# Query chunks of batches 3 to 7 transposed by DMA in a fused linear-attention and FFN kernel

## The chip, the cores and the metric

The kernel runs on one core of a Trainium2 chip. The metric is the device time of one execution, in microseconds (us). Five runs of the kernel before give a median of 259.1 us (258.8 to 259.48). Besides them there is one profiled execution; every duration below comes from it.

## The reference

A cosformer attention (linear attention with cosine and sine weights) is followed by a multiplicative feed-forward network:

```python
def phi(x, c, s):                      # q, k, v: (8 batches, 8 heads, 576, 64)
    r = np.maximum(x, 0.0)
    return np.concatenate([r * c, r * s], axis=-1)
q_p, k_p = phi(q, cos_w, sin_w), phi(k, cos_w, sin_w)
kv = np.einsum('bhsf,bhsd->bhfd', k_p, v)
z = np.sum(k_p, axis=2)
num = np.einsum('bhsf,bhfd->bhsd', q_p, kv)
den = np.einsum('bhsf,bhf->bhs', q_p, z)[..., None] + 1e-06
x = (num / den).transpose(0, 2, 1, 3).reshape(4608, 512)
out = ((x @ w1) * (x @ w2) @ w3) @ w_out          # widths 1024, 1024, 1024, 512
```

## The kernel before, in words

The 576 tokens of a batch are cut into five chunks, four of 128 rows and chunk 4 of 64. `order_of(b)` gives their order: 0, 1, 2, 3, 4 for even batches and 4, 0, 1, 2, 3 for odd ones. The FFN runs over the 4608 tokens in nine tiles of 512; w3 and w_out are multiplied into one matrix `w34b` during the first of them.

The main loop runs over the FFN tiles, t = 0 to 8; I call one turn a stage. `ffn_groups(t)` is a generator which emits TensorE work of tile t in up to 24 pieces of four matmuls (some 0.9 us each): eight pairs of products with w1 and w2 (L438, evacuated at L475 on ScalarE and L479 on VectorE), then four output blocks (L484, L490, stores at L423). After each piece the units of the slot of that number are emitted, so the slots set the order in which the other work joins each engine's queue. The schedule is manual: each engine executes its instructions in the order in which they were emitted, and waits on semaphores where one needs another's result.

In stage t (from t = 2 on; stages 0 and 1 have slot tables of their own) three batches are in work:

- Batch t+3 is loaded by DMAs that GpSimd issues (L112, L114), with a cast to bf16. K, q and v are put into slots 1, 8 and 15.
- Batch t+2 gets its features: `prep_k`, `prep_q`, `prep_v` for each chunk, spread over slots 0 to 22, in stage 1 (batch 3) over slots 6 to 23. The cosine half is made on VectorE (L251), the sine half on ScalarE (L255), the copy of v on GpSimd (L275).
- Batch t+1 gets its attention (`attention_at`): `kv_chunk` in slots 0 to 4 (L283), then for each chunk `num` (L341, with the normalization on VectorE, L349 to L351) and `x_tr` in slots 6, 8, 11, 14, 17. For batches 2 and later `x_tr` is a DMA transpose that SP issues (L373); it writes the normalized rows into `xT`, the FFN's input.

`num` needs the query features with the feature dimension on the partitions: `qpT`. There are two ways to get there. By TensorE: `q_tr` makes eight transposes into PSUM (L314, one for each head), and VectorE copies the result to `qpT` (L316). That happens in the batch's own attention stage, in slots 2, 4, 7, 10 and 13 of stage b-1. By DMA: `prep_q` issues a transpose from SP (L269) right after the chunk's features, in stage b-2. `dma_q(b)` lists the chunks of batch b that go by DMA; `attention_at` gives the others to `q_tr`.

Before the change `dma_q` gives no chunk for batches 0 to 2, chunks 2 and 3 for batch 3, chunks 2, 3, 4 for batches 4 and 6, chunks 1, 2, 3 for batch 5, and all five for batch 7. SP's queue holds these transposes and those of `x_tr`, in the order of the slots.

Because batches have 576 rows and FFN tiles 512, `xT` of tile t takes rows from two batches. Tile 3 takes the last rows of batch 2 and chunks 4, 0 and 1 of batch 3; tile 4 takes chunks 2 and 3 of batch 3 and chunks 0 and 1 of batch 4; tile 5 the other three of batch 4 and chunks 4 and 0 of batch 5.

`qpT` has two buffers (L243), and so have the feature tiles and the loaded tiles; `xT` has three.

Of the kernel before, what the change touches and what calls it, by code (L numbers as in the profile page):

```python
# [68 lines left out]
def kernel(  # L69
# [12 lines left out]
    B = q.shape[0]  # L82
# [141 lines left out]
    def order_of(b):  # L224

        return [0, 1, 2, 3, 4] if b % 2 == 0 else [4, 0, 1, 2, 3]

    def dma_q(b):

        return order_of(b)[5 if b < 3 else 3 if b == 3 else 2 if b < B - 1 else 0:]  # L230

    feat = {}

# [31 lines left out]
    def prep_q(b, c):  # L265
        features(b, feat_of(b)[1], raw[b, "q"], c)
        if c in dma_q(b):
            R = ROWS[c]
            nc.sync.dma_start_transpose(out=att_of(b)["qpT"][:, :, ds(columns_of(b, c), R)],  # L269
                                        in_=feat[b][1][:R, c].rearrange("p h f -> p (h f)"))  # L270
# [110 lines left out]
    def attention_at(b, slots, kv, tr, nu, xt):  # L381

        each = list(enumerate(order_of(b)))
        for i, c in each:
            slots[kv[i]].append(lambda c=c, i=i: kv_chunk(b, c, i))
            if c not in dma_q(b):
                slots[tr[i]].append(lambda c=c: q_tr(b, c))
        for i, c in each:
            if xt[i] > nu[i]:
                slots[xt[i]].append(lambda c=c: x_tr(b, c))  # L390
        for i, c in each:
            slots[nu[i]].append(lambda c=c: num(b, c))
            if xt[i] == nu[i]:
                slots[xt[i]].append(lambda c=c: x_tr(b, c))
# [238 lines left out]
```

## Time and profile before

| | |
|---|---|
| median of five runs | 259.1 us (258.8 to 259.48) |
| the profiled execution | 259.03 us, its span 257.3 us |
| mean granted TensorE clock | 0.995 |
| transposes by TensorE for `qpT` (L314) | 184, 23 chunks, with eight more at L327 |
| copies PSUM to `qpT` (L316) | 20 on VectorE, 12.4 us in total |
| DMA transposes to `qpT` (L269) | 16, issue 1.26 us, 2.7 / 4.1 / 6.1 us to landing (min/median/max) |
| DMA transposes to `xT` (L373) | 30, issue 1.19 us, 2.3 / 3.1 / 7.7 us to landing |
| DMA moved | 37.1 MB, mean 144 GB/s |

In what follows the span starts at 0. PE is TensorE's matmul side, PEld its weight loads, DVE VectorE, ACT ScalarE, POOL GpSimd, SP SyncE. A busy row of PE includes the tail of its pipeline, so the time that a group of matmuls costs is read from the start of the group to the start of the next one. "To landing" is the time from the issue of a DMA to its completion. The DMA share of a stretch can exceed 1, since packets of one engine overlap.

### The profile page before, as it was taken

Reading aid. Unit: us, or ns where it says so; the run is one execution under the profiler, and the core shown is the slowest. Engines: PE = TensorE matmul, PEld = TensorE weight load, DVE = VectorE, ACT = ScalarE, POOL = GpSimd, SP = SyncE. Lnnn points to the kernel's source line nnn. Section 1 sums busy time; section 2 is a strip of 40 time slices with the busy share of each in tenths; the row PEclk is TensorE's granted clock in tenths of the full one; section 3 lists DMA queues with packets and bytes.
Section 4 is the critical chain, followed back from the end, with each engine's and each line's share of the span. In section 5 each row is a group of like instructions: output and inputs, shape, how many; then the busy total and the mean of one; then the engine's idle time right before and its main releaser. Section 6 shows DMA issues by size and latency. Waiting matters only on the chain.

```text
span 257.3 us, 5053 instructions
## 1 busy us (share of the span) xinstructions
PE 247.0 (96%) x1934; PEld 135.2 (53%) x1967; DVE 146.1 (57%) x346; ACT 128.0 (50%) x219; POOL 85.5 (33%) x147
## 2 busy tenths in 40 slices
PE   8889999999999999999999999999999999999992
PEld 3478555656565455446544654555455544444441
DVE  6775655847879549824871787278526614303310
ACT  2675316727966546555655465646523233323321
POOL 7665144530760483048305900610230031022000
PEclk9999999999999999999999999999999999999998
DMA  7999999999999599999999999826490252024025
GB/s 195 183 194 203 207 206 201 198 199 198 237 160 138 102 201 171 173 171 162 192 150 181 176 195 135 179 50 131 94 194 13 54 123 70 0 44 122 1 44 120
DMA packets 68025, 37.10 MB, mean 144 GB/s; under 512 B 35617, under 2 KB 64545, under 8 KB 68001
## 3 DMA queue, kind: packets, MB, share of 16 engines
q0 software_dynamic: 35488, 27.20, 66.0%
q1 hardware_dynamic: 32352, 9.44, 21.9%
q8 instruction: 15, 0.25, 0.4%
q10 hardware_dynamic: 160, 0.13, 0.2%
q14 instruction: 10, 0.07, 0.1%
HBM read 38.80 MB, written 9.44 MB: 187 GB/s over the span
## 4 chain that ended last, share of the span: by engine, by line
PE 89%; DMA 3%; ACT 2%; issue 2%; DVE 1%; POOL 1%; ACTq 0%; POOLq 0%
PE ffnps L438 47%; PE ffnps L484 22%; PE ffnps L218 5%; PE pst L314 4%; PE pnum L341 4%; PE pnum L283 3%; DMA qs<-in_q_dram 3%; PE pst L206 1%; PE pst L377 1%; ACT kp L255 1%; POOL vs L120 0%; ACT qpT L317 0%; PE ffnps L501 0%; ACT osb L503 0%; DVE xblk L351 0%
## 5 line engine op out<-in xcount | busy, mean ns | idle before, releaser
L479 DVE TENSOR_TENSOR abT<-asb,ffnps 128x512 bf16<-128x512 bf16 x68 | 46.4, 682 | 64.1 <-PE ffnps L438 57.6
L438 PE MATMUL ffnps<-xT,w1b 128*128 128x512 bf16 (+2 forms) x312 | 74.3, 357 | 0.9 <-DVE xT L379 0.3
L438 PE MATMUL ffnps<-xT,w2b 128*128 128x512 bf16 (+2 forms) x306 | 73.2, 356 | 0.5
L475 ACT CAST asb<-ffnps 128x512 bf16<-128x512 f32 x68 | 39.8, 586 | 63.0 <-PE ffnps L438 55.5
L484 PE MATMUL ffnps<-w34b,abT 128*128 128x512 bf16 x273 | 63.3, 379 | 0.4
L423 POOL DMA_DIRECT2D out_dram<-osb x42 | 22.3, 536 | 120.1 <-ACT osb L490 120.1
L438 PEld LDWEIGHTS <-w1b 128*128 128x128 bf16 x320 | 28.9, 98 | 27.5 <-issue 0.8
L484 PEld LDWEIGHTS <-abT 128*128 128x128 bf16 x280 | 26.5, 98 | 30.3 <-DVE abT L479 0.4
L438 PEld LDWEIGHTS <-w2b 128*128 128x128 bf16 x320 | 27.5, 97 | 22.7
L490 ACT COPY osb<-ffnps 128x512 f32<-128x512 f32 x35 | 20.5, 586 | 37.8 <-PE ffnps L484 36.7
L255 ACT ACTIVATE qp<-qs,sinv 128x512 bf16<-128x512 bf16 (+2 forms) x40 | 28.1, 717 | 1.2 <-DMA qs<-in_q_dram 1.2
L351 DVE TENSOR_TENSOR xblk<-pnum,den 128x512 bf16<-128x512 f32 (+1 forms) x39 | 26.9, 691 | 1.4
L255 ACT ACTIVATE kp<-ks,sinv 128x512 bf16<-128x512 bf16 (+1 forms) x35 | 24.9, 722 | 0.0
L341 PEld LDWEIGHTS <-qpT 128*128 128x128 bf16 x320 | 15.1, 98 | 8.8 <-DVE xblk L351 0.9
L251 DVE TENSOR_SCALAR qp<-qs,cosv 128x512 bf16<-128x512 bf16 (+1 forms) x40 | 18.2, 462 | 0.5 <-DMA qs<-in_q_dram 0.5
L275 POOL COPY va<-vs 128x512 bf16<-128x512 bf16 (+1 forms) x30 | 18.4, 644 | 0.0
L341 PE MATMUL pnum<-kvs,qpT 128*128 128x65 bf16 x312 | 16.4, 194 | 0.4 <-DVE kvs L289 0.3
L283 PEld LDWEIGHTS <-kp 128*128 128x128 bf16 x280 | 12.7, 98 | 5.2
L316 DVE COPY qpT<-pst 128x1024 bf16<-128x1024 bf16 (+1 forms) x20 | 12.4, 618 | 4.8 <-PE pst L314 4.7
L218 PE MATMUL ffnps<-woutb,w3T 128*128 128x512 bf16 x61 | 15.0, 379 | 0.1
L314 PEld LDWEIGHTS <-qp 128*128 128x128 bf16 x184 | 12.0, 98 | 4.7
L283 PE MATMUL pnum<-va,kp 128*128 128x65 bf16 x280 | 14.1, 193 | 0.0
(81 smaller groups left out, 178.8 us busy)
## 6 DMA issues: line engine op xcount, KB each, us to landing
out_dram<-osb POOLq DMA_DIRECT2D x16, 256.0 KB, 3.8
out_dram<-osb POOLq DMA_DIRECT2D x24, 128.0 KB, 3.1
qs<-in_q_dram POOLq DMA_DIRECT2D x9, 256.0 KB, 8.0
ks<-in_k_dram POOLq DMA_DIRECT2D x7, 320.0 KB, 7.7
qs<-in_q_dram POOLq DMA_DIRECT2D x7, 320.0 KB, 8.2
vs<-in_v_dram POOLq DMA_DIRECT2D x7, 320.0 KB, 10.0
w3b<-in_moe_w_dram POOLq DMA_DIRECT2D x8, 256.0 KB, 12.7
ks<-in_k_dram POOLq DMA_DIRECT2D x7, 256.0 KB, 8.3
```

The source lines that it names most:

```text
L218: nc.tensor.matmul(acc[:, :], lhsT=w3T[:, lc, :], rhs=woutb[:, lc, :], start=(lc == 0), stop=(lc == 7))
L255: nc.scalar.activation(out=dst[:R, c, 0:n, D:F], in_=src[:R, 0:n, c, :], func=ACTF.Relu, scale=sinv[:R, at:at + 1], bias=0.0)
L283: nc.tensor.matmul(kvt[:, h // 4, ds((h % 4) * 65, 65)], lhsT=kp[:, c, h, :], rhs=va[:, c, h, 0:D + 1], start=(i == 0 and h % 4 == 0), sto ...
L314: nc.tensor.transpose(pst[:, h, :], qp[:, c, h, :], identb[:])
L341: nc.tensor.matmul(nt[:, h // 4, ds((h % 4) * 65, 65)], lhsT=qpT[:, h, ds(at, 128)], rhs=kvs[:, h, :], start=True, stop=True)
L351: nc.vector.tensor_tensor(out=xblk[rows], in0=n4[:, :, :, 0:D], in1=den[rows].unsqueeze(3).to_broadcast([R, 2, 4, D]), op=ALU.mult)
L423: on.dma_start(out=rows[:, :, cols], in_=osb[64 * i:64 * i + rows.shape[0], :, cols])
L438: nc.tensor.matmul(out, lhsT=w[:, kc, ts(jc, 128)], rhs=x[:, kc, tok], start=(kc == 0), stop=(kc == 3))
L475: nc.scalar.copy(out=asb[:], in_=aT[:, :])
L479: nc.vector.tensor_mul(out=abT[:, jc, :], in0=asb[:], in1=bT[:, :])
L484: nc.tensor.matmul(ops[:, :], lhsT=abT[:, jc, ts(ms, 128)], rhs=w34b[:, jc, :], start=(jc == 0), stop=(jc == 7))
L490: nc.scalar.copy(out=osb[:, ms % 2, :], in_=ops[:, :])
```

## The change

`dma_q` lists all five chunks for batches 3 to 7. Batches 0 to 2 stay with TensorE.

```diff
     def dma_q(b):
 
-        return order_of(b)[5 if b < 3 else 3 if b == 3 else 2 if b < B - 1 else 0:]
+        return order_of(b)[5 if b < 3 else 0:]
```

So nine chunks change their path: 4, 0 and 1 of batch 3, 0 and 1 of batch 4, 4 and 0 of batch 5, 0 and 1 of batch 6. For each of them `prep_q` issues a DMA transpose on SP in stage b-2, and `q_tr` with its eight transposes and its VectorE copy drops out of stage b-1. Nothing else is edited.

## The prediction

> **What bounds the kernel now.** I read the page first (busy times, then the row of granted clock), then the busy times of TensorE (PE) stage by stage, then single pieces of PE's timeline, and last the landings of the transposes that SP issues.
>
> The page:
>
> ```profile
> span 257.3 us, 5053 instructions
> PE 247.0 (96%) x1934; PEld 135.2 (53%) x1967; DVE 146.1 (57%) x346; ACT 128.0 (50%) x219; POOL 85.5 (33%) x147
> ...
> PEclk9999999999999999999999999999999999999998
> DMA  7999999999999599999999999826490252024025
> ```
>
> PE is busy in 96% of the span at a granted clock of nine tenths or more throughout; no other engine comes near. The DMA row is the only other full one, up to about slice 27 (174 us), and that is the stretch in which the change adds DMA work.
>
> Busy times in the five stages t = 2 to 6 (a row is: stretch, length, PE, PEld, DVE, ACT, POOL, clock, DMA share, GB/s). I took the borders from the first matmul of each stage on PE's timeline:
>
> ```profile
> 90.45:115.06 24.61, 24.40 (x197) 13.28 (x200) 16.29 (x37) 13.59 (x23) 10.23 (x17) 1.00 1.21 176
> 115.06:139.23 24.17, 24.01 (x190) 12.83 (x192) 15.05 (x36) 13.60 (x23) 10.20 (x17) 1.00 1.09 176
> 139.23:163.40 24.17, 23.96 (x189) 12.82 (x192) 15.12 (x36) 13.59 (x23) 9.15 (x15) 1.00 1.15 166
> 163.40:187.57 24.17, 24.01 (x190) 12.84 (x192) 15.31 (x35) 13.60 (x23) 5.73 (x11) 1.00 0.54 112
> 187.57:210.85 23.28, 23.07 (x173) 11.94 (x176) 10.74 (x24) 7.31 (x13) 3.15 (x7) 1.00 0.39 83
> ```
>
> In every stage PE is busy for all but about 0.2 us. The lengths of the rows hold the price list of this change. They follow the number of query chunks that PE transposes in the stage: three in stage 2 (batch 3), two in stages 3, 4 and 5 (batches 4, 5, 6), none in stage 6 (batch 7). 24.61 less 24.17 is 0.44 for one chunk, and 24.17 less 23.28 is 0.89 for two.
>
> PE's timeline in stage 4 (start, length, what):
>
> ```profile
> 142.33 0.61 PE L314 MATMUL pst<-identb,qp 128*128 128x128 bf16 x8
> 142.78 0.42 PE L283 MATMUL pnum<-va,kp 128*128 128x65 bf16 x8
> ```
>
> A chunk is eight transposes. The 0.61 includes the tail of the pipeline; the next group starts 0.45 us later, and 0.45 is what PE gives up. It agrees with the differences of the rows.
>
> **What the change removes.** It hits batch 3 chunks 4, 0, 1; batch 4 chunks 0, 1; batch 5 chunks 4, 0; batch 6 chunks 0, 1: nine chunks. Off PE go 9 x 8 = 72 transposes, 9 x 0.45 = 4.05 us, all on the engine that sets the end: 1.35 in stage 2 and 0.9 in each of stages 3, 4, 5. Off VectorE (DVE) go nine copies of L316, seven at 0.69 and two at 0.41, 5.7 us. DVE is busy for 15 to 16 us of 24, so that is worth nothing. No matmul loses cover between its two uses of a buffer: the removed groups of slots 2 and 4 stand ahead of kv chunks, not between the last kv chunk and the first `num`, and the one of slot 7 (stage 2 only) stands between two `num`s which in stages 3 to 6 follow each other without it, and without a gap. Stage 6 already runs in this form, but with half the ACT work and no loads; for ACT and DVE at the faster pace in stages 2 to 5 I charge nothing (13.6 of 23.3 us; if a late `asb` copy does show, 0.1 us or so per stage, 0.4 in all).
>
> **What it adds.** Nine DMA transposes on SP's queue, seven of 256 KB and two of 128 KB, each about 1.25 us of SP. SP then issues ten in a stage, some 12.2 us of 24. Queued behind them on SP are the transposes of `xblk` (L373) that build the FFN's input, and nothing else that anyone waits for. In the order of the slots the five of a stage are q, x, q, x, q, x, x, q, x, q. The first q of stage 2 has its features at 95.3 (DVE's 1.64 us piece from 93.66), five us ahead of the first x at 100.24. The second has them at 100.5, and the x behind it becomes ready at 102.7, so one issue of 1.25 us fits between. Waiting on SP: zero.
>
> Readers of the added `qpT` columns are the `num` matmuls one stage later, from slot 6 on (98.65 in stage 2, against features done by 84.2 in stage 1). Between issue and landing the q transposes take 2.7 to 6.1 us. With over 8 us to spare for each chunk I charge nothing.
>
> What is left is the DMA engines. The trace of before has no q transpose inside a burst of loads, so I bound it. Transposes alone, in stage 5 (q first, then x):
>
> ```profile
> DMA to landing us min/median/max: 3.2/3.2/3.2
> ...
> DMA to landing us min/median/max: 2.4/2.4/2.5
> ```
>
> So 128 KB more (q is 256 KB, x 128) costs 0.8 us, and a whole q transpose 1.6 us of the engines' time. With several queued at once the landings of stage 2 give another figure. The stage's transposes issued at 100.24, 102.73, 104.54 and 105.95 took 7.7, 6.1, 5.2 and 5.7 us, so they landed at 107.9, 108.8, 109.7 and 111.7: 512 KB in 3.7 us after the first, 1.87 us for 256 KB. The packets' own busy time is lower: from 180 to 184 us 1398 packets held the queue for 42.3% of 16 engines in 4 us, 19 ns each, so 1.24 us for 1024 packets. I take 1.6, from the landings, with 1.24 and 1.87 as ends.
>
> Who is late then? Each FFN stage needs its whole `xT`. From the slots, `xT` of stages 4 and 5 is complete some 7 us ahead (the transposes of 126.87 and 151.04 took 5.6 and 5.5), later ones more. Only that of stage 3 is tight: its last piece is chunk 1 of batch 3, issued at slot 11 of stage 2:
>
> ```profile
> L373 SPq DMA_TRANSPOSE xT<-xblk x1: 1582/1582/1582, 106.0 to 106.0; - x1
> ...
> DMA to landing us min/median/max: 5.7/5.7/5.7
> ```
>
> and PE reads it here:
>
> ```profile
> 115.06 1.03 PE L438 MATMUL ffnps<-xT,w1b 128*128 128x512 bf16 x4
> ```
>
> It lands at 105.95 + 5.7 = 111.65, 3.4 us ahead. In the new kernel PE arrives 1.35 us earlier (113.7), which leaves 2.05, and two q transposes (3.2 us) have joined the queue ahead of it. If the landing is set by the backlog, it moves to 114.9, and PE stalls for 1.15 us. If it is set by its own issue, which also moves 1.35 earlier, 3.2 fits into 3.4, and PE doesn't stall. I take the middle, 0.55. Ends: 0, and 2 x 1.87 - 2.05 = 1.7.
>
> **Two rules of the Trainium skill against these rows.** "VectorE: DVE Perf Modes", in "The three transpose paths" and its rules, speaks against the change: a full 128x128 block goes to TensorE where PSUM will do as destination, at 390 ns against 1309 by DMA. The rows: 0.45 / 8 = 56 ns on PE, and 3.2 / 8 = 400 ns by DMA. With the page's figures the PE time given back would be an estimate of 72 x 0.39 = 28 us, and the DMA side 94 us in one file. With the rows it is 4.05 and about 13 (8 full-sized equivalents x 1.6), spread over 90 us and beside PE. The direction of the rule holds per block; it doesn't decide here, since only PE's side is on the path.
>
> "DMA: Bandwidth & Descriptors", in "Queues, rings and completion order", has each DMA engine go round its queues packet by packet. By that the first q transpose of stage 2, issued at 95.3 among loads that last to 108.4 (the last issued at 97.61, landing after 10.8), would be through before the x transposes come, and take its time from the loads, which aren't needed before 115: one transpose ahead, 1.6 us, no stall. The row says otherwise: a 64 KB piece issued at 100.24 landed at 107.9, when the loads did. By the row both added transposes stand ahead: the 1.15 above. That is the other reason for a middle value.
>
> **Rivals.**
> No stall (0.27): round robin holds, or the landing follows its issue. 259.1 - 4.05 = 255.05.
> The mid case (0.46): a stall of 0.3 to 1.7 us at the start of stage 3, gain 2.35 to 3.75, 255.35 to 256.75; centre 0.55, or 255.6.
> Another engine takes over, or a longer stall eats most of it (0.13, about 0.04 of it within 0.2% of no change): ACT or DVE can't follow, or the stall is 1.7 to 4 us; 256.8 to 259.6. For it: the DMA share of 1.21 in stage 2. Against: no gap on PE names ACT or DVE in stages 2 to 6.
> Slower (0.14): in a burst of loads the transposes go one at a time, each at the 5.2 us that the q of 104.54 took from issue to landing. Then the two ahead cost 10.4, the piece of `xT` lands at 122, PE stalls for 8.35 us, and the sum is 259.1 - 4.05 + 8.35 = 263.4. It decides from a stall of 4.05 us on, that is from 3.05 us per added transpose. Against: four of them landed in 3.7 us, overlapped; and the stages after it have 7 us of slack. That the change doesn't do what it says I hold excluded: batch 7 already goes this way.
>
> **How the numbers follow.** The profiled execution took 259.03 with a span of 257.3; 1.7 lies around it. 257.3 - 4.05 + 0.55 = 253.8, plus 1.7 is 255.5. The median of the runs is 0.07 above the profiled one: 255.6. The range runs from just under no stall, 254.9, over the mid case to a stall of 2.3, 257.3, which leaves out the slower case and part of the long stalls. A measurement tells about 0.2% (0.5 us) from no change. Faster 0.82, within 0.04, slower 0.14.
>
> **What would show it.** PE should hold 72 transposes less (L314 from x184 to x112), and L316 eleven instead of twenty. Stages 3, 4, 5 should read 23.3 each, as stage 6 does now; stage 2 too, 23.3. Any stall should stand before the first L438 of stage 3, released by the DMA `xT<-xblk`. I am wrong if PE waits for `qpT`, if loads of k, q or v come late for the features, or if stages 4 to 6 begin with a gap as well.

## The result, and the profile after

The 28 runs of the changed kernel took 256.0 to 264.06 us, median 260.18; the 47 runs of the kernel before 258.64 to 260.48, median 259.1. A comparison of the shorter runs alone (those within 1.5% of the lowest, 11 of the 28) has a ratio of 0.9949, interval 0.9934 to 0.9965, about 257.8 us; but the runs of before spread over 1.8 us and those of the changed kernel over 8.1, so the spread belongs to the change, and both figures count. The forecast of 255.6 (254.9 to 257.3) holds neither. In its shorter runs the kernel is 1.3 us faster; 19 of the 28 lie above the median of before.

The profiled execution took 257.19 us. The page (busy times, granted clock, DMA share by slice):

```profile
span 255.4 us, 4929 instructions
PE 243.2 (95%) x1863; PEld 130.9 (51%) x1895; DVE 141.0 (55%) x337; ACT 127.6 (50%) x219; POOL 85.3 (33%) x147
...
PEclk9999999999999999999999999999999999999999
DMA  7999999999999899999999999976890452024025
```

The 72 transposes and nine DVE copies are gone as announced (L314 x112, L316 x11). The stages 2 to 6, by their first matmuls (rows as in the prediction: stretch, length, PE, PEld, DVE, ACT, POOL, clock, DMA share, GB/s):

```profile
90.65:115.78 25.13, 23.28 (x174) 11.84 (x176) 14.63 (x34) 14.08 (x24) 11.01 (x19) 1.00 1.24 186
115.78:139.07 23.29, 23.13 (x174) 11.95 (x177) 14.15 (x34) 12.91 (x22) 9.42 (x16) 1.00 1.34 180
139.07:162.57 23.50, 23.23 (x174) 11.87 (x177) 13.79 (x34) 13.52 (x24) 9.15 (x15) 1.00 1.30 183
162.57:185.84 23.27, 23.11 (x173) 11.94 (x177) 13.94 (x34) 13.48 (x23) 5.72 (x11) 1.00 0.82 158
185.84:209.12 23.28, 23.12 (x174) 11.93 (x176) 10.74 (x24) 7.31 (x13) 3.15 (x7) 1.00 0.49 83
```

PE's busy time is 23.1 to 23.3 in all five, as stage 6 had it before. Stage 2 lasts 25.13 instead of 24.61 - 1.35 = 23.26. Stage 4 is 0.23 longer than 24.17 - 0.90 = 23.27, and stage 3 0.02. So -4.05 + 1.87 + 0.23 + 0.02 = -1.93, and the five lengths together went from 120.40 to 118.47. The 1.87 stands in one place; PE's timeline, with the idle time and its releaser in brackets:

```profile
111.77 2.32 PE L484 MATMUL ffnps<-w34b,abT 128*128 128x512 bf16 x10
115.78 1.04 PE L438 MATMUL ffnps<-xT,w1b 128*128 128x512 bf16 x4 [1.69 <-DMA xT<-xblk]
```

That is the first matmul of stage 3 waiting for the transposed chunk 1 of batch 3, the piece that the prediction named; I call it the x piece of stage 3. Why it was that late is on SP's timeline (start, length of the issues, count):

```profile
95.66 1.99 SPq L269 DMA_TRANSPOSE qpT<-qp  x1
99.62 1.23 SPq L373 DMA_TRANSPOSE xT<-xblk  x1
100.96 3.08 SPq L269 DMA_TRANSPOSE qpT<-qp  x1
104.13 2.15 SPq L373 DMA_TRANSPOSE xT<-xblk  x1
106.38 4.07 SPq L269 DMA_TRANSPOSE qpT<-qp  x1
110.54 3.22 SPq L373 DMA_TRANSPOSE xT<-xblk  x2
```

The piece was issued at 110.54; before, at 105.95. An issue of a q transpose, 1.2 us elsewhere, here takes 3 and 4 us: SP stays inside the instruction, which I call the hold, while transposes issued earlier have not landed and the loads of the stage (its burst) are under way. The two issued at 95.66 and 100.96 landed only after 11.4 and 10.9 us, and the last load of the burst after 13.9 instead of 10.8.

The order counts as well. In all 18 profiles the transposes landed in the order in which SP issued them. The q transpose issued at 106.38 landed at 115.27, the x piece behind it at 115.73. In that order the x piece can't be there before the q transposes ahead of it, however early SP issues it.

Three further profiled runs of the same kernel, listed below, gave 257.46, 263.37 and 258.09 us. The long one tells what a run over 260 is made of. Its stages 2 to 6:

```profile
90.23:115.94 25.71, 23.45 (x178) 11.86 (x176) 14.64 (x34) 14.07 (x24) 11.57 (x20) 1.00 1.27 183
115.94:140.88 24.94, 24.94 (x176) 12.49 (x177) 13.80 (x34) 12.90 (x22) 8.84 (x15) 0.93 1.29 182
140.88:167.06 26.18, 23.45 (x178) 11.86 (x177) 13.89 (x34) 14.07 (x24) 10.97 (x19) 1.00 1.38 152
167.06:191.99 24.93, 24.93 (x177) 12.50 (x178) 13.22 (x33) 12.90 (x22) 3.80 (x8) 0.93 0.94 145
191.99:215.26 23.27, 23.27 (x177) 11.94 (x176) 10.75 (x24) 7.30 (x13) 3.14 (x7) 1.00 0.39 83
```

Two stages end with a gap (2 and 4), and the two behind them run at a granted clock of 0.93. The gaps on its PE timeline, before stages 3 and 5:

```profile
115.94 0.82 PE L438 MATMUL ffnps<-xT,w1b 128*128 128x512 bf16 x3 [2.26 <-DMA xT<-xblk]
...
167.06 0.81 PE L438 MATMUL ffnps<-xT,w1b 128*128 128x512 bf16 x3 [2.73 <-issue]
```

The second has no releaser by the profile; the transposed piece that stage 5 lacks, issued at 155.22, landed at 166.97, 0.09 us ahead of the matmul. And right behind the first gap (clock in the eighth column):

```profile
115.90:120.50 4.60, 4.56 (x28) 2.17 (x29) 1.19 (x2) 1.81 (x3) 3.99 (x7) 0.63 1.09 244
120.50:124.00 3.50, 3.50 (x38) 2.01 (x37) 0.69 (x1) 1.45 (x4) 2.12 (x4) 1.00 1.51 149
```

A mean of 0.63 over 4.6 us is 3.4 us at half the clock. This costs 1.66 us in stage 3 (24.94 against 23.28) and 1.66 again in stage 5. So this run is 259.03 - 4.05 + 2.26 + 2.73 + 3.3 = 263.27 against 263.37 measured. The Trainium skill ("TensorE: Matmul & The Clock Gate", "Why this matters for your kernels") warns of PE-idle gaps over about 3 us. Here gaps of 2.26 and 2.73 did it, and gaps of 1.0 to 1.8 us in the other profiles did not.

The length of a gap doesn't decide it alone, though: in one run below (all three pairs held back) a gap of 2.73 us was followed by the full clock. In all traces, changes of the clock lie whole multiples of 3.41 us apart. So I cut two profiles at these steps: the run above, before and after its second change, and the other run around its gap of 2.73 us.

```profile
164.91:168.32 3.41, 1.26 (x13) 0.77 (x14) 0.00 (x0) 0.24 (x2) 3.08 (x6) 1.00 1.41 146
168.32:171.73 3.41, 3.41 (x17) 1.50 (x15) 0.94 (x2) 1.61 (x3) 0.22 (x1) 0.50 1.22 211
...
157.96:161.37 3.41, 1.66 (x8) 0.57 (x6) 1.10 (x3) 1.25 (x3) 0.00 (x0) 1.00 1.44 174
161.37:164.79 3.42, 2.44 (x19) 1.26 (x20) 1.84 (x6) 0.24 (x1) 0.00 (x0) 1.00 1.16 217
164.79:168.20 3.41, 3.36 (x16) 1.56 (x16) 0.00 (x0) 1.74 (x4) 1.71 (x3) 1.00 1.02 189
```

The first gap left PE idle for 3.41 - 1.26 = 2.15 us of one step. The second fell across two steps and left 1.75 and 0.98. Over all gaps with a fall of the clock, PE was idle for 2.15 to 2.85 us of the step before it; no step with at most 1.82 us idle, at full clock, was followed by one. Six gaps with a fall are few, and what lies between 1.82 and 2.15 wasn't measured.

### The profile page after: what moved, and what is told of

It is laid out like the page before. It is cut to its first block, busy times and chain, and to the rows that moved or that the text cites. A ratio compares the mean times of both kernels' runs of the same rounds, so it can differ in the third digit from the quotient of the medians.

```text
span 255.4 us, 4929 instructions
## 1 busy us (share of the span) xinstructions
PE 243.2 (95%) x1863; PEld 130.9 (51%) x1895; DVE 141.0 (55%) x337; ACT 127.6 (50%) x219; POOL 85.3 (33%) x147
## 3 DMA queue, kind: packets, MB, share of 16 engines
q1 hardware_dynamic: 40832, 11.54, 30.2%
## 4 chain that ended last, share of the span: by engine, by line
PE 82%; DMA 9%; DVE 2%; ACT 2%; issue 1%; POOL 1%; ACTq 0%; POOLq 0%
PE ffnps L438 48%; PE ffnps L484 19%; DMA qs<-in_q_dram 7%; PE ffnps L218 4%; PE pnum L341 3%; PE pnum L283 3%; DMA xT<-xblk 2%; PE pst L314 2%; PE pst L206 1%; ACT kp L255 1%; PE pst L377 1%; DVE xblk L351 1%; DVE va L275 0%; POOL vs L120 0%; DVE qpT L316 0%
## 5 line engine op out<-in xcount | busy, mean ns | idle before, releaser
L484 PE MATMUL ffnps<-w34b,abT 128*128 128x512 bf16 x274 | 63.3, 379 | 0.3
L484 PEld LDWEIGHTS <-abT 128*128 128x128 bf16 x280 | 26.5, 98 | 30.3 <-DVE abT L479 0.4
L341 PEld LDWEIGHTS <-qpT 128*128 128x128 bf16 x320 | 15.1, 98 | 8.8 <-DVE xblk L351 0.9
L341 PE MATMUL pnum<-kvs,qpT 128*128 128x65 bf16 x312 | 16.4, 194 | 0.3 <-DVE kvs L289 0.3
L251 DVE TENSOR_SCALAR kp<-ks,cosv 128x512 bf16<-128x512 bf16 (+1 forms) x35 | 12.5, 370 | 0.1
L349 DVE TENSOR_SCALAR den<-pnum 128x8 f32<-128x8 f32 (+1 forms) x39 | 6.3, 162 | 9.0 <-PE pnum L341 8.6
## 6 DMA issues: line engine op xcount, KB each, us to landing
out_dram<-osb POOLq DMA_DIRECT2D x16, 256.0 KB, 4.7
qs<-in_q_dram POOLq DMA_DIRECT2D x9, 256.0 KB, 11.3
vs<-in_v_dram POOLq DMA_DIRECT2D x7, 320.0 KB, 11.4
w3b<-in_moe_w_dram POOLq DMA_DIRECT2D x8, 256.0 KB, 12.8
ks<-in_k_dram POOLq DMA_DIRECT2D x7, 256.0 KB, 10.3
```

Of the source, the lines that this page charges most:

```text
L251: nc.vector.tensor_scalar(out=dst[:R, c, :, 0:D], in0=src[:R, :, c, :], scalar1=0.0, scalar2=cosv[:R, at:at + 1], op0=ALU.max, op1=ALU.mult)
L341: nc.tensor.matmul(nt[:, h // 4, ds((h % 4) * 65, 65)], lhsT=qpT[:, h, ds(at, 128)], rhs=kvs[:, h, :], start=True, stop=True)
L484: nc.tensor.matmul(ops[:, :], lhsT=abT[:, jc, ts(ms, 128)], rhs=w34b[:, jc, :], start=(jc == 0), stop=(jc == 7))
```

## The experiments

Three theories were set against each other. **Backlog**: SP's issues are held while loads drain; that delays the x piece of stage 3, and what is carried on delays other pieces in stages 3 and 4. (Hold and order of landing go together in it: no run has the one without the other.) **Amount**: only the additional bytes in the stretch count, wherever they stand. **Arrival**: PE comes earlier at landings that always varied. All kernels are edits of the changed one; the figures in brackets behind a median are the lowest and the highest run, and a ratio compares the shorter runs with the kernel before, which had medians of 259.09 to 259.12 beside them. Lines that a diff leaves out are marked by "...".

**Batch 3 alone.**

```diff
-        return order_of(b)[5 if b < 3 else 0:]
+        return order_of(b)[5 if b < 3 else 0 if b in (3, B - 1) else 2:]
```

> Only batch 3's three chunks change their path; batches 4, 5, 6 stay as before. Queue theory (the x transpose of batch 3's chunk 1 is late because batch 4's two added q transposes stand ahead of it on SP, which holds its issue while loads drain): none stands ahead here, so the piece of xT lands at 111.7 or earlier, PE arrives at 113.7, no stall: 259.1 - 1.35 = 257.75, runs as close together as before (within 0.5 us of the median). Amount theory (it is the additional DMA work in the stretch, wherever it stands): 0.64 of 1.15 MB added ahead of stage 3, stall about half of the 1.9 us, 258.7. Arrival theory (PE arrives 1.35 us earlier at a landing that varies anyway): a stall in part of the runs, single runs up to 260.

Measured 257.53 (257.38 to 257.6), ratio 0.9941 (0.9928 to 0.9954). No wait of PE for a DMA beyond the start. Arrival falls: PE came at 113.78 and the piece was there.

**All but batch 4.**

```diff
-        return order_of(b)[5 if b < 3 else 0:]
+        return order_of(b)[5 if b < 3 else 2 if b == 4 else 0:]
```

> Batches 3, 5, 6, 7 go wholly by DMA, batch 4's chunks 0 and 1 stay on TensorE: seven of the nine chunks. Queue theory: 7 x 0.45 = 3.15 us saved, no stall before stage 3, 255.95, and the runs within 0.5 us of each other. Amount theory: five of the nine added transposes lie in other stages already, so a stall of over 1 us somewhere stays, 257 or more, runs spread. Arrival theory: as the changed kernel, a gap before stage 3 in part of the runs, spread over 3 us and more.

Measured 256.68 (255.96 to 257.0), ratio 0.9905 (0.9892 to 0.9917). Between the expectations: the profiled run, 255.96, has no gap, which is what backlog gave for stage 3, but three of four runs are 0.6 to 1.0 longer. Seven of nine chunks can be had nearly whole. Over these four runs batch 4's two make most of the spread; but batches 5 and 6 alone, below, spread over 2.4 us in eight runs.

**Batch 4's two behind the x piece.**

```diff
...
+            if b == 4 and c < 2:
+                held.append((b, c))
+            else:
+                q_dma(b, c)
...
+            if t == 2:
+                slots[11] += [lambda c=c: q_dma(4, c) for c in (0, 1)]
```

> As the changed kernel, with one edit: the q transposes of batch 4's chunks 0 and 1 are issued right behind the x transpose of slot 11 of stage 2 instead of in slots 1 and 6. Same number of transposes, same bytes. Queue theory: the x piece is issued at about 104.6 as its normalization ends and lands before 113.7; no gap before stage 3, all 4.05 us stay: 255.05, runs close together. The two deferred q land by about 116, their first reader comes at about 120. Amount theory: the bytes are the same, so the gap stays at 1.5 to 2 us and the spread too: 257 or more.

Two runs at 255.48 and 255.51, two at 260.7 and 261.51. The x piece was issued at 104.96 and the gap before stage 3 is gone in all that the profile shows, with the same bytes; it landed at 112.42, again right behind the q transpose ahead of it (111.96). But a new gap appears where I had expected none (profile of the run at 261.51; the added lines shift the line numbers, so that L350 here is L341 and L493 is L484):

```profile
153.51 1.89 PE L493 MATMUL ffnps<-w34b,abT 128*128 128x512 bf16 x8
158.66 0.62 PE L350 MATMUL pnum<-kvs,qpT 128*128 128x65 bf16 x8 [3.25 <-DMA qpT<-qp]
```

That is the last `num` of batch 5. Its q transpose, the last one emitted in stage 3, was issued at 145.08, inside the load burst of stage 4, and landed 13.5 us later. The delay of SP's queue had been handed on from stage 2 through stage 3. So my account of backlog was right for the first place and incomplete: it needs the amount as well. In the two shorter runs, which have no profile, nothing shows whether that gap was there.

**Loads of stage 2 later.**

```diff
-                for g, name in ((1, "k"), (8, "q"), (15, "v")):
+                for g, name in ((1, "k"), (20, "q"), (20, "v")) if t == 2 else ((1, "k"), (8, "q"), (15, "v")):
```

> As the changed kernel, with one edit: in stage 2 the loads of q and v of batch 5 are emitted in slot 20 instead of 8 and 15, behind a store that GpSimd has to wait for, so that they are issued at about 110 instead of 95 to 98. Queue theory with loads as what holds SP: SP issues each q transpose in about 1.3 us instead of 2.0, 3.1 and 4.1, the x piece is issued at about 104.6, no gap before stage 3: 255.05, unless the later loads make stage 3 late (they land at about 120; v is wanted by GpSimd from 117 on, by TensorE only in stage 4; q features from 116 on, which ScalarE would wait for: up to 4 us). If SP is held by the transposes alone: the gap of about 1.9 us stays.

Measured 264.73 (261.61 to 266.12), ratio of the three shorter runs 1.0142 (1.0117 to 1.0166). As a time, a miss. In stage 2 it did what backlog said: without q and v loads in the queue SP's last two q issues ahead of the x piece took 1.6 and 1.25 us, the x piece went out at 104.76, and there is no gap before stage 3. But the burst now met stage 3: features came late (PE waited 1.4 us for ScalarE), an xT piece and a qpT chunk were late by 2.8 us each.

**Batch 4 alone.**

```diff
-        return order_of(b)[5 if b < 3 else 0:]
+        return order_of(b)[5 if b < 3 else 3 if b == 3 else 2 if b in (5, 6) else 0:]
```

> Only batch 4's chunks 0 and 1 change their path. Backlog theory (SP's issues are held while loads drain; the hold delays the x piece of stage 3 and, where it is carried on through stages 3 and 4, the last q chunk of batch 5): the two stand ahead of the x piece, which lands at about 115.5 as in the changed kernel, but PE arrives at 115.06, not earlier; a gap of 0 to 1 us before stage 3, then no more: 259.1 - 0.9 + 0.5 = 258.7, runs within 1.5 us. If the place of the two didn't matter: 258.2 and close runs.

Measured 258.15 over 22 runs (257.58 to 259.51), ratio 0.997 (0.9961 to 0.9979). Both theories were near. SP shows the hold without help from other batches: the q transposes ahead of the x piece took 2.99, 1.79 and 3.94 us, the piece went out at 110.15 and landed at 114.85, 0.3 ahead of PE in the profiled run. So small a margin would let single runs slip; of the longer runs there is no profile.

**No loads in stages 2 to 4.**

```diff
             if t + 3 < B:
+                for name in "kqv":
+                    raw[t + 3, name] = raw[t + 1, name]
+            if False:
                 for g, name in ((1, "k"), (8, "q"), (15, "v")):
                     slots[g].append(lambda name=name: load(t + 3, name))
```

> As the changed kernel, but the loads of q, k and v of batches 5, 6 and 7 are left out (stages 2, 3, 4 load nothing; those batches' features are made from the tiles of batches 3 and 4, so their output is not theirs). Backlog theory: without loads to drain, SP issues each transpose in 1.2 to 1.4 us, no gap before stage 3, none in stage 4: 255.05, runs within 0.5 us. If ten transposes in a stage are too many for SP by themselves: issues of 3 to 5 us stay, and the time stays at 256 to 264.

Measured 255.37 (255.3 to 255.44), ratio 0.9855 (0.9842 to 0.9867). The order on SP and the number of transposes are those of the changed kernel; its SP timeline:

```profile
100.77 1.25 SPq L269 DMA_TRANSPOSE qpT<-qp  x1
102.11 1.23 SPq L373 DMA_TRANSPOSE xT<-xblk  x1
103.45 1.25 SPq L269 DMA_TRANSPOSE qpT<-qp  x1
104.79 3.60 SPq L373 DMA_TRANSPOSE xT<-xblk  x2
```

Every issue is short (the two of the last row 1.2 us each, with a wait between them), all the gaps and the spread are gone, the 4.05 us are there but for 0.3. This is the clearest of the runs: ten transposes in a stage are not too many for SP, it is their meeting with the loads. The kernel leaves out loads that its result needs, so this is a measurement and not a way to win the time.

**The x piece by TensorE.** In `x_tr` chunk 1 of batch 3 takes the PSUM way, in slot 13.

```diff
-        if b >= 2:
+        if b >= 2 and (b, c) != (3, 1):
...
-                             nu=(6, 8, 11, 14, 17), xt=(6, 8, 11, 14, 17))
+                             nu=(6, 8, 11, 14, 17), xt=(6, 8, 13 if t == 2 else 11, 14, 17))
```

> As the changed kernel, but the x piece that came late (chunk 1 of batch 3, tile 3 of the FFN) is transposed by TensorE in slot 13 of stage 2 (four transposes, 0.22 us, and a ScalarE copy). Backlog theory: the gap before stage 3 is gone, 259.1 - 4.05 + 0.22 = 255.3 in the better runs; the runs still spread to 261, because the last q chunk of batch 5 is issued some 8 us late in stage 4 in part of them. If the gap before stage 3 is the only cause of the spread: all runs at 255.3 within 0.5 us.

Six runs from 255.58 to 260.29, median 256.81. As backlog said: the best run is 0.3 short of the full gain, the spread stays. Its profile, that of the best run, has no gap; the gap before stage 3 isn't the only cause of the spread.

**Batches 5 and 6 alone.**

```diff
-        return order_of(b)[5 if b < 3 else 0:]
+        return order_of(b)[5 if b < 3 else 3 if b == 3 else 2 if b == 4 else 0:]
```

> Only batches 5 and 6 change (chunks 4, 0 and 0, 1); stage 2 is as before. Backlog theory: no backlog comes over from stage 2, so the last q chunk of batch 5 goes out before the load burst of stage 4: 259.1 - 1.8 = 257.3, runs within 1 us. If stage 3 and 4 make the backlog by themselves: a gap before the last num of batch 5, runs up to 261.

Eight runs, 256.72 to 259.12, median 257.35. The median is the expected one, the spread twice what I gave backlog. Its profile has the gap before stage 5, not before batch 5's last `num`:

```profile
163.28 1.02 PE L438 MATMUL ffnps<-xT,w1b 128*128 128x512 bf16 x4 [0.29 <-DMA xT<-xblk]
```

Batch 6's two transposes do in stage 4 what batch 4's do in stage 2: the x piece of chunk 0 of batch 5 landed at 163.04; before, at 156.57.

**All three pairs held back.** As above, for batches 4, 5 and 6.

```diff
+    HELD = (4, 5, 6)
...
+            if t + 2 in HELD:
+                slots[11] += [lambda c=c: q_dma(t + 2, c) for c in order_of(t + 2)[:2]]
```

> As the changed kernel, but in each of stages 2, 3 and 4 the first two q transposes (batches 4, 5, 6) are issued behind the x transpose of slot 11 instead of in slots 1 and 6. Backlog theory: no x piece has a q of its own stage ahead of it in the load burst; if what has to move after the burst fits into the rest of the stage, all 4.05 us stay: 255.05 to 255.5 with close runs. If it doesn't fit (five q at 1.4 us, five x at 0.7 and 1 MB of stores at about 5 us make 15.5 us for some 14 us between the end of one burst and the end of the next), the last q chunks slip into the next burst, as in the run with only batch 4's held back, and the runs spread to 261.

Two runs at 254.94, four from 259.48 to 262.42: the second branch. In the longest run, two `num`s waited 2.85 and 2.73 us for qpT, and behind the first of the two gaps the clock fell to half for 3.4 us. Order alone doesn't save it when three stages in a row get more.

**Batches 3 and 5.**

```diff
-        return order_of(b)[5 if b < 3 else 0:]
+        return order_of(b)[5 if b < 3 else 0 if b in (3, 5, B - 1) else 2:]
```

> Only batches 3 and 5 change (chunks 4, 0, 1 and 4, 0). Their transposes are added in stage 1 and stage 3, each followed by a stage without additions, in which a backlog can drain; the x pieces of the FFN tile that follows stage 3 have slack. Backlog theory: 259.1 - 5 x 0.45 = 256.85, runs within 0.6 us. If any addition to a stage with loads spreads the runs: as with batches 5 and 6 alone, runs up to 2.4 us above the lowest.

Measured 256.57 (256.51 to 256.64), ratio 0.9904 (0.9892 to 0.9917): backlog, with each addition followed by a stage in which it can drain.

**Batches 4 and 6 held back, batch 5 as before.**

```diff
-        return order_of(b)[5 if b < 3 else 0:]
+        return order_of(b)[5 if b < 3 else 2 if b == 5 else 0:]
...
+    HELD = (4, 6)
...
```

> Batches 3, 4, 6, 7 wholly by DMA, batch 5's chunks 4 and 0 on TensorE; the first two q transposes of batches 4 and 6 are issued behind the x transpose of slot 11. Seven of nine chunks, additions in stages 1, 2 and 4, none in stage 3. Backlog theory: 259.1 - 3.15 = 255.95, no gap before stages 3 and 5, the backlog of stage 2 drains in stage 3: runs within 1 us. If the amount alone decides: as with all but batch 4, 256.7 and a spread of 1 us or more.

Nine runs, median 255.93; seven within 255.67 to 256.18, one at 257.13 and one at 259.48. The expected time, and a rest of the spread that I can't place, since the profile is of a run without a gap.

**The changed kernel again.** No edit.

> The changed kernel once more, for another profile of it. Backlog theory: a longer run than the one profiled shows a gap of over 2 us before stage 3, before the last num of batch 5 in stage 4, or before stage 5, and a stretch at half the TensorE clock right behind the gap; a shorter run shows none of these. If the spread comes from elsewhere: a longer run without such a gap.

18 runs, 256.6 to 267.64, median 259.09, ratio of the shorter ones 0.9978 (0.9957 to 0.9998). The profiled run, 258.34, is longer than the first and has two gaps: 1.03 us before stage 3 and 1.82 before stage 5, both without a change of clock. So neither is over 2 us, as I had expected of a longer run.

> The changed kernel once more, for a profile of one of its longer runs. Backlog theory: a run over 260 us shows a gap of over 2 us ended by a DMA transpose (before stage 3 or 5 by xT, or before a late num by qpT), and right behind it one or two stretches of about 3.4 us at half the TensorE clock. A run over 260 without such a gap would refute it.

257.46; gaps of 1.01 and 0.99 us in the same places, two instead of the one at most that the next two texts give for a run below 258.

> The same kernel for a further profile: as for the look before, a gap that a DMA transpose ends, and half a clock behind it, if the run is over 260 us; below 258 us one gap of 1 to 2 us at most.

263.37; the run shown above, with 2.26 and 2.73 and the half clock behind each.

> The same kernel for a further profile, with the same expectation: over 260 us a gap of over 2 us ended by a DMA transpose and a stretch at half the clock, below 258 us one gap of 1 to 2 us at most.

258.09; gaps of 1.77 and 1.16 us.

**Batches 3, 5, 6, with batch 6's two behind the x piece.**

```diff
-        return order_of(b)[5 if b < 3 else 0:]
+        return order_of(b)[5 if b < 3 else 2 if b == 4 else 0:]
...
+    HELD = (6,)
...
```

> Batches 3, 5, 6, 7 wholly by DMA, batch 4's chunks 0 and 1 on TensorE (seven of nine chunks), and in stage 4 the two added q transposes of batch 6 are issued behind the x transpose of slot 11. Backlog theory: the x piece of stage 5 has no added q ahead of it, and what is carried on lands in stage 5, which has no loads: 259.1 - 3.15 = 255.95, runs within 0.6 us, where the same seven chunks in the order of the changed kernel gave 255.96 to 257.0. If only the number of chunks counted: again a spread of 1 us and a median near 256.7.

Measured 256.09 (255.63 to 256.29), ratio 0.9882 (0.9866 to 0.9899), no wait of PE for a DMA after the start. The same seven chunks in the changed kernel's order spread over 1.04 us with a median of 256.68; with four runs each and intervals that overlap (0.9892 to 0.9917 there), the gain of the order is likely, not shown. Every run lies below every run of the kernel before, and below all but two of the 28 of the changed kernel.

## Why the prediction was wrong, point by point

- **What PE gives back: right.** Without loads the stages read 23.28 each, and the whole gain but 0.3 us came. (The clock row of before ends with an 8, which I read as nine tenths or more; it is the last slice, outside the stages.)
- **The place of the first stall: right.** Before stage 3, released by `xT<-xblk`.
- **"Waiting on SP: zero", and with it the size of the stall: the step that failed first.** I charged each added issue 1.25 us and found room for one between two x issues; so half of the 0.55 us rested on a landing that follows an issue 1.35 us earlier than before. In the burst the three q issues ahead took 2.0, 3.1 and 4.1 us, and the x piece went out 4.6 us later than before; without loads it went out at 104.79, where I had it. With that the case without a stall was void. The other case, the backlog, was the right one and too small: the landing came 4.06 us later than before, not 3.2, and the stall, by the length of stage 2, was 1.87 us, where the backlog case had 1.15 and the forecast the middle, 0.55.
- **The engines' time for a q transpose, 1.6 us: in line with the loads, and used in the wrong way.** The end of the loads moved from 108.4 to 111.7, 3.3 for two. But the x piece waits for the passage of everything ahead of it on its own queue, and it landed at 115.73, beyond my upper end of 111.65 + 2 x 1.87 = 115.4. The gap before stage 3 was 1.0 to 2.3 us over five profiles.
- **"`xT` of stages 4 and 5 is complete some 7 us ahead": wrong for stage 5.** I compared landings of the old trace and didn't put batch 6's two transposes into the burst of stage 4, ahead of the piece that stage 5 needs. It landed 0.1 us ahead of the matmul in the first profile and ended a gap of 1.0 to 2.7 in the four others. The same for qpT: of "over 8 us to spare" 0.2 to 3.1 us were left for the last chunk of batch 5 in four of the five profiles of the changed kernel, and less than nothing in those of three edits of it (batch 4's two behind the x piece, loads of stage 2 later, all three pairs held back). In the four profiles at the full clock the two gaps come to 1.7 to 2.9 us together, against the 0.55 of the sum.
- **A term that was missing: the clock.** Of the seven gaps of 2.26 to 3.25 us in the profiles, six were followed by a stretch at half the clock, in the run shown another 1.66 us for each. It makes 263 out of 260.
- **A single number for a kernel whose end now waits for DMA.** Before, PE had no gap in the stages, and the runs agreed within 0.7%. With the slack used up, the runs differ by the gaps that they have. The shortest run, 256.0, lies in the middle case (255.35 to 256.75), but no profile is of such a run, so that may be luck; a forecast of the median had to count the gaps of a typical burst.
- **The rules weighed.** By the packet-wise round I had the first q transpose through before the x pieces come; it took 11.4 us, as long as the loads. The round itself shows in the trace, though. No packet of a transpose moved from 95.6 to 99.5, some 4 us from the issue on; from 102 to 109 us the queue of the loads (q0) and that of the transposes (q1) moved equally many packets (packets, MB, share):

```profile
q0 software_dynamic: 1585, 0.88, 88.9%
q1 hardware_dynamic: 1585, 0.39, 46.1%
```

Over the run q1 moved 40832 packets instead of 32352, so 1060 for each of eight full q transposes. At 1585 in 7 us that is an estimate of 4.7 us for one that shares the engines with the loads, three times what I charged (the q transpose issued at 100.96 landed 3.9 us behind the transpose ahead of it, and the loads thinned out before its end). So the counts agree with the rule, and my use of it failed: a turn at every packet is not a way past the burst when each q transpose has a thousand packets, starts late, and the x piece stands behind three of them.

What stays open: why one of nine runs with batches 4 and 6 held back took 259.48, and what makes one run's burst drain 2 us slower than another's; no run here separates that. What limits the number of transposes that SP can have under way was only seen in the length of its issues, not measured by itself. Whether the x piece would have landed earlier without the hold, with the same transposes ahead of it, is open too: putting it ahead, or leaving out the loads, changes hold and backlog together.

## What to carry to other kernels

When a transfer is moved to a queue, cost the queue at the moment when it is fullest: an issue that takes 1.2 us on a quiet chip held SP for 3 to 6 us behind loads, and everything behind it on that queue waited too. Before work is taken off the critical engine, list each piece with its landing and its reader, add the new backlog to every stage that inherits it, and keep urgent small pieces ahead of bulky ones that have time. Take part of such a change if the rest uses up the slack: five or seven chunks of nine, in the right order, gave runs within 0.7 us of each other and medians of 256.6 and 256.1 (four runs each; another seven had one run of nine at 259.48), where nine gave 256 to 268 us.

## What the runs showed of the hardware that I had not expected

- An issue of a DMA transpose lasted 1.2 us with free queues and up to 5.8 us in the first profile (L269, 1192 to 5817 ns), 2.0 at most without the loads.
- Transposes landed in the order of their issue in all 18 profiles, and in a burst their queue and that of the loads moved packet for packet (1585 each in 7 us).
- A PE gap of 2.26 us was followed by 3.41 us at half the clock; one of 3.25 us by 6.83 us, which began within it; a gap of 2.73 us once was and once wasn't; eight gaps of 1.0 to 1.8 us by none.
